# First loads reordered over two queues, the attention state split into two tiles, and a new instruction order in a fused attention and FFN kernel

## The chip, the cores and the metric

The kernel runs on one core of a Trainium2 chip. A core has five engines with instruction streams of their own: TensorE (PE in the profile, with PEld for its weight loads), VectorE (DVE), ScalarE (ACT), GpSimd (POOL) and SyncE (SP). SP, ACT and POOL also issue DMAs; "SPq" and "ACTq" in a timeline are such issues. The metric is the time of one execution on the device in microseconds (us); the time of a kernel is the median of several runs.

## The reference

Four batches, four heads, 1088 tokens, head size 32. The attention is linear: each query and key becomes 64 features, the outer product of two sketches of size 8, and there is no softmax over pairs of tokens. Its output, 4352 tokens of 128 channels, goes through an FFN of 2048 hidden units with a squared relu.

```python
def phi(x):
    a = np.einsum('rd,bhsd->bhsr', S1, x)
    b = np.einsum('rd,bhsd->bhsr', S2, x)
    return np.einsum('bhsi,bhsj->bhsij', a, b).reshape(*x.shape[:-1], r * r)
q_p, k_p = (phi(q), phi(k))
kv = np.einsum('bhsf,bhsd->bhfd', k_p, v)
z = np.sum(k_p, axis=2)
num = np.einsum('bhsf,bhfd->bhsd', q_p, kv)
den = np.einsum('bhsf,bhf->bhs', q_p, z)[..., None] + 1e-06
attn = num / den
...
h = x @ w_in
r = np.maximum(h, 0.0)
g = r * r
return (g @ w_out).astype(np.float32)
```

## The kernel before

**Operations and order.** The kernel first describes its work as named operations (`add`, each with the engines that may run it and the operations it needs). A long text, `PLAN` (lines 31 to 105), then lists every operation once with its engine and, where it needs one, a PSUM bank (`b0` to `b7`), a pair of banks (`h0` to `h6`, where `h0` is banks 0 and 1) or a buffer. `Graph.emit` issues them in that order. So each engine has a fixed list, and runs it strictly in order; semaphores between engines are set automatically from what an operation reads and writes. A DMA that is listed on SP, ACT or POOL is issued when that engine's list gets to it.

**Names.** `S0`, `S1`: loads of the two sketch matrices. `ldk`, `ldq`, `ldv` plus batch: loads of keys, queries, values. `warm`: one small activation that makes ACT load its table. `ST`, `SK`, `SQ0`, `SQ1` (DVE), `SR0`, `SR1` (ACT): the sketch matrices transposed and masked in the forms that later matmuls use. `zero`, `z0`, `z1`, `mk`, `ident`, `iota`: constants and cleared tiles. `heat`: matmuls on zeros that keep TensorE busy until there is data.

**Attention of a batch.** Keys: `tk` (DVE transpose, L393), `ksk` (PE sketches, L400), `kt` (DVE transpose back, L410 and L415), `kp` (feature products on DVE or POOL, L424), `vp` (values copied beside a column of ones, ACT or POOL, L382), `kv` (PE, L436: the state, 64 features by 33 columns for each head, in a PSUM bank). `kve` (L451) copies the state from PSUM into the SBUF tile `st`, in four pieces of 64 partitions: two head positions in each of two arrangements, the second with the partition halves swapped. Queries of batch 0 and of the first part of batch 1: `tq` (DVE transpose, L457), `qr` (PE, L478), `qa` (ACT copy of one factor, L487), `qp` (DVE product, L492), `num` (PE, L521), `mx` (DVE: add eps, reciprocal, multiply; L532 to L535), `tx` (PE transpose, L546), `xe` (copy to `xT`, L551). The rest of the queries go through `qr2`/`qr3` (L562), `ab` (ACT, L567), `rdA` (DMA, L575, the copies named `Aq`), `qb` (PE, L589), `qp` (L596), `den` (PE, L618), `dc` (ACT), `d1` (DMA, L633), `rc` (DVE, L638 and L639), `d2` and `d3` (DMA, L643 and L648, the reciprocals go out to DRAM and come back spread over partitions), `num` (L661) and `xm` (DVE, L668), which writes `xT`.

**FFN.** Ten blocks of tokens (`BLOCKS`: 256, 256, seven of 512, 256). For block n, `m1.n.m` (PE, L697) makes hidden units, `r.n.m` is the relu (ACT, L708, or DVE, L710), `g.n.m` the square (DVE, L721, or ACT, L719), `m2.n.m` (PE, L728) sums over hidden units in a bank, `oe` (DVE, L736) transposes the result into an `osb` buffer, and four `st` DMAs (L746) store it. FFN matmuls of early blocks are interleaved with the attention of later batches.

**POOL.** It clears tiles, waits for a query piece (`gate`, L303), issues the four weight loads (`w_in0`, `w_in1`, `w_out0`, `w_out1`), then runs `vp` and `kp`, and small copies (`gate2`, `pace2k`, `pace3k`) that hold back the loads of the next batch.

Of the kernel before, what the change touches and what calls it, by code (L numbers as in the profile page):

```python
# [36 lines left out]
heat15:PE:b6 heat16:PE:b6 heat17:PE:b6 heat18:PE:b6 heat19:PE:b6 heat20:PE:b6 heat21:PE:b6 heat22:PE:b6
heat23:PE:b6 heat24:PE:b6 heat25:PE:b6 heat26:PE:b6 heat27:PE:b6 heat28:PE:b6 ksk0.0:PE:h0 kt0.0:DVE
heat29:PE:b6 heat30:PE:b6 ksk0.1:PE:h2 ldv0.4:ACT ldv0.5:ACT ldv0.6:ACT ldv0.7:ACT SR0:ACT
SR1:ACT heat31:PE:b6 heat32:PE:b6 heat33:PE:b6 heat34:PE:b6 heat35:PE:b6 heat36:PE:b6 qr0.0:PE:h0:h4  # L40
kt0.1:DVE kp0.0:DVE tq0.8:DVE tq0.16:DVE vp0.0:ACT qa0.0.0:ACT:A0 qp0.0.0:DVE qa0.0.1:ACT:A1
w_in0:POOL w_in1:POOL qr0.8:PE:h2:h6 kv0.0:PE:b0 qp0.0.1:DVE qa0.8.0:ACT:A0 qp0.8.0:DVE qa0.8.1:ACT:A1
qp0.8.1:DVE vp0.4:ACT qr0.16:PE:h1:h3 qa0.16.0:ACT:A1 qa0.16.1:ACT:A0 kp0.7:DVE qp0.16.0:DVE kp0.4:POOL
kv0.4:PE w_out0:POOL w_out1:POOL kv0.7:PE kve0.3:ACT kve0.2:ACT SQ0:DVE gate2:POOL
ldk1.0:SP ldv1.0:SP kve0.1:ACT qp0.16.1:DVE qr0.24:PE:h1:h5 ldv1.1:SP ldv1.2:SP kve0.0:DVE
num0.0:PE:b0 mx0.0:DVE:den0 num0.8:PE:b3 num0.16:PE:b4 tx0.0:PE:b0 qa0.24.0:ACT:A0 qa0.24.1:ACT:A1 qp0.24.0:DVE
qp0.24.1:DVE xe0.0:ACT m1.0.0:PE:h0 mx0.8:DVE:den0 ldv1.3:SP mx0.16:DVE:den1 m1.0.1:PE:h5 tx0.8:PE:b7
xe0.8:DVE r.0.0:ACT:r0 g.0.0:DVE:g0 m1.0.2:PE:h2 tx0.16:PE:b4 xe0.16:DVE r.0.1:ACT:r1 g.0.1:DVE:g1
# [52 lines left out]
m2.8.7:PE g.9.0:DVE:g1 m2.9.0:PE:b5 r.9.2:DVE:r2 r.9.3:DVE:r0 g.9.1:ACT:g0 g.9.2:ACT:g2 m1.9.4:PE:h1  # L101
oe8:DVE:osb0 st8.3584.0:SP m2.9.1:PE m2.9.2:PE g.9.3:DVE:g1 r.9.4:ACT:r1 m2.9.3:PE g.9.4:DVE:g0
m2.9.4:PE st8.3584.1:SP st8.3584.2:SP st8.3584.3:SP oe9:DVE:osb1 st9.4096.0:SP st9.4096.1:SP st9.4096.2:ACT
st9.4096.3:ACT
"""


# [683 lines left out]
```

## Time and profile before

| | |
|---|---|
| three runs, median (lowest to highest) | 111.31 us (110.62 to 111.45) |
| the profiled execution: its time | 112.11 us |
| the profiled execution: span from first to last instruction | 110.1 us |
| first FFN matmul starts | 17.59 us |
| last FFN matmul ends | 105.87 us |
| granted TensorE clock, mean | 1.00 |
| busy: PE, DVE, ACT, POOL | 96.6, 88.8, 85.7, 25.0 us |

A row of a timeline has the start and the time of an instruction (or of a run of like instructions, with their number at the end), the engine, the line, the operation, what it writes and reads and in what shape, and in square brackets how long the engine had stood idle before it and what released it. Matmuls are pipelined and their ends are modelled, so that their rows can overlap. Rows with "q" after the engine are DMA issues or waits of the engine's sequencer.

### The profile page before, as it was taken

To read this page: it belongs to the slowest core of one execution; us is meant where nothing else is said; L and a number is where in the kernel's file an instruction comes from. 1 tells how busy PE (TensorE), PEld (TensorE's weight loads), DVE (VectorE), ACT (ScalarE), POOL (GpSimd) and SP (SyncE) were. 2 spreads that over 40 slices of the span, in tenths; PEclk is the share of its full clock that TensorE was granted. 3 is DMA by queue.
4 is the path that set the end of the run, shared out by engine and by line. 5 is a ranking of instruction groups with operands and counts; after the bars stand their busy time and mean duration, and the time that the engine had idled before them with its cause. 6 is when DMAs were issued, how large, how long until landed. Compare 5 with 4: busy or idle time off the path is not lost.

```text
span 110.1 us, 3711 instructions
## 1 busy us (share of the span) xinstructions
PE 96.6 (88%) x1524; PEld 58.9 (54%) x1539; DVE 88.8 (81%) x153; ACT 85.7 (78%) x108; POOL 25.0 (23%) x37
## 2 busy tenths in 40 slices
PE   5976988998697979997998999999999999999940
PEld 5533976885463546444564543455554554557620
DVE  2479739989997687687959884989998989998940
ACT  2244755998994898899658999999999898999910
POOL 7007700025983990087000000000000000000000
PEclk9999999999999999999999999999999999999999
DMA  0984999931993990964206577005093633502343
GB/s 6 297 192 131 154 187 305 222 129 46 307 270 55 312 261 33 202 131 90 95 10 161 119 191 190 0 6 88 8 227 63 118 53 55 95 6 36 60 85 58
DMA packets 27544, 13.91 MB, mean 126 GB/s; under 512 B 20232, under 2 KB 25352, under 8 KB 27528
## 3 DMA queue, kind: packets, MB, share of 16 engines
q1 hardware_dynamic: 25760, 12.26, 46.4%
q0 software_dynamic: 576, 1.05, 5.8%
q10 hardware_dynamic: 1192, 0.37, 1.4%
q8 instruction: 12, 0.20, 0.7%
q14 instruction: 4, 0.03, 0.1%
HBM read 10.17 MB, written 2.27 MB: 113 GB/s over the span
## 4 chain that ended last, share of the span: by engine, by line
PE 35%; DVE 16%; SPq 13%; issue 11%; DMA 9%; ACT 8%; POOL 4%; DVEq 0%; ACTq 0%
PE psum L697 9%; DVE g L721 8%; SPq L746 8%; PE psum L728 7%; PE psum L436 5%; ACT r L708 5%; PE psum L478 4%; DMA vin<-in_v_dram 4%; PE psum L521 3%; DVE r L710 3%; POOL kp L424 3%; DMA qin<-in_q_dram 3%; PE psum L618 2%; ACT g L719 2%; DMA out_dram<-osb 2%
## 5 line engine op out<-in xcount | busy, mean ns | idle before, releaser
L708 ACT ACTIVATE r<-psum 128x1024 bf16<-128x1024 f32 (+1 forms) x57 | 54.4, 1017 | 5.5 <-PE psum L697 2.8
L697 PE MATMUL psum<-xT,w_in 128*128 128x512 bf16 (+1 forms) x154 | 37.9, 348 | 2.5 <-DVE r L710 1.0
L728 PE MATMUL psum<-g,w_out 128*128 128x512 bf16 (+1 forms) x152 | 38.2, 346 | 1.8 <-DVE st L451 0.6
L721 DVE TENSOR_TENSOR g<-r 128x2048 bf16<-128x2048 bf16 (+2 forms) x31 | 31.8, 1045 | 1.6 <-ACT r L708 0.6
L697 PEld LDWEIGHTS <-w_in 128*128 128x128 bf16 x160 | 21.3, 145 | 14.2 <-issue 3.9
L728 PEld LDWEIGHTS <-w_out 128*128 128x128 bf16 x160 | 14.6, 98 | 14.4 <-issue 3.4
L424 POOL TENSOR_TENSOR kp<-ks 128x768 f32<-128x768 f32 x10 | 16.2, 1632 | 7.1 <-PE psum L697 5.7
L719 ACT ACTIVATE g<-r 128x2048 bf16<-128x2048 bf16 (+1 forms) x10 | 17.4, 1746 | 0.2 <-DVE r L710 0.2
L710 DVE TENSOR_SCALAR r<-psum 128x1024 bf16<-128x1024 f32 (+1 forms) x12 | 14.0, 1175 | 1.4 <-PE psum L697 0.7
L436 PEld LDWEIGHTS psum<-vp,kp 128*32 128x32 f32 (+1 forms) x504 | 7.3, 114 | 4.3 <-issue 3.7
L436 PE MATMUL psum<-vp,kp 128*32 128x33 f32 (+1 forms) x504 | 8.2, 202 | 1.6 <-DVE qp L492 0.7
L492 DVE TENSOR_TENSOR qp<-psum,A 128x256 f32<-128x256 f32 (+2 forms) x14 | 6.2, 474 | 2.4 <-ACT A L487 2.4
L487 ACT COPY A<-psum 128x256 f32<-128x256 f32 (+2 forms) x14 | 5.3, 421 | 2.7 <-PE psum L478 1.7
L293 PE MATMUL psum<-zero 128*128 128x128 bf16 (+1 forms) x36 | 6.0, 347 | 1.3 <-DVE mk L246 1.2
L596 DVE TENSOR_TENSOR qp<-psum,Aq 128x544 f32<-128x544 f32 x8 | 5.4, 719 | 1.6 <-ACT r L708 1.5
L393 DVE STREAM_TRANSPOSE kT<-kin 128x1088 f32<-128x1088 f32 (+2 forms) x5 | 5.4, 1072 | 1.6 <-DMA kin<-in_k_dram 1.6
L736 DVE STREAM_TRANSPOSE osb<-psum 128x512 f32<-128x512 f32 (+1 forms) x10 | 6.2, 625 | 0.5 <-PE psum L728 0.5
L478 PE MATMUL psum<-qT,SR 32*64 32x128 f32 (+2 forms) x224 | 6.1, 304 | 0.6 <-issue 0.4
L457 DVE STREAM_TRANSPOSE qT<-qin 128x1088 f32<-128x1088 f32 (+2 forms) x6 | 5.5, 914 | 0.2 <-DMA qin<-in_q_dram 0.2
L293 PEld LDWEIGHTS <-zero 128*128 128x128 bf16 x37 | 3.7, 135 | 2.7 <-DVE mk L246 1.2
L382 POOL COPY vp<-vin 128x640 f32<-128x640 f32 (+1 forms) x4 | 3.1, 786 | 9.0 <-DMA vin<-in_v_dram 9.0
L478 PEld LDWEIGHTS psum<-qT,SR 32*64 32x64 f32 x224 | 3.5, 131 | 2.8 <-issue 0.9
(58 smaller groups left out, 65.3 us busy)
## 6 DMA issues: line engine op xcount, KB each, us to landing
Aq<-ab SPq DMA_DIRECT2D x16, 136.0 KB, 2.4
kin<-in_k_dram SPq DMA_DIRECT2D x3, 544.0 KB
qin<-in_q_dram SPq DMA_DIRECT2D x3, 544.0 KB
recq<-scd SPq DMA_DIRECT2D x8, 136.0 KB, 2.7
out_dram<-osb SPq DMA_DIRECT2D x16, 64.0 KB, 1.9
vin<-in_v_dram SPq DMA_DIRECT2D x6, 144.0 KB, 5.9
vin<-in_v_dram SPq DMA_DIRECT2D x6, 128.0 KB
w_in<-in_moe_w_in_dram POOLq DMA_DIRECT2D x2, 256.0 KB, 4.7
```

What stands on the lines that cost most here:

```text
L293: nc.tensor.matmul(at(hb)[:, 0:n], zero[:, 0:128], zero[:, 0:n], start=True, stop=True)
L424: eng.tensor_tensor(out=kp[i][:, 4 * a0 : 4 * a1].rearrange("p c (a b) -> p c a b", b=R), in0=t[:, :, 1][:, :, None, :].to_broadcast([128, ...
L436: nc.tensor.matmul(t[p : p + KM, 33 * pr : 33 * pr + 33], kp[i][:, 4 * a0 + 2 * na * pr + 2 * (j - a0) + m, p % 64 : p % 64 + KM], vp[i][: ...
L478: nc.tensor.matmul(at(hbs[h // 2])[p : p + 64, 512 * u + 256 * x : 512 * u + 256 * x + n], SR[32 * h : 32 * h + 32, x, m].rearrange("p a b ...
L492: nc.vector.tensor_tensor(out=qp[i][:, pr, t0 : t0 + 2 * n].rearrange("p (u s) -> p u s", u=2), in0=at(hb).rearrange("p (u s) -> p u s", u ...
L697: nc.tensor.matmul(at(hb)[:, step * w : step * w + N], w_in[:, 128 * E * (ct // E) : 128 * E * (ct // E + 1)].rearrange("p (c e) -> p e c" ...
L708: nc.scalar.activation(o, h, ACTF.Relu)
L710: nc.vector.tensor_scalar_max(o, h, 0.0)
L719: nc.scalar.activation(at(gb)[:, 0 : Q * W * N], r, ACTF.Square)
L721: nc.vector.tensor_tensor(out=at(gb)[:, 0 : Q * W * N], in0=r, in1=r, op=ALU.mult)
L728: nc.tensor.matmul(at(ob)[:, 0:N], w_out[:, ct, :], at(gb)[:, lo : lo + N], start=(ct == 0), stop=(ct == CT - 1))
L746: dma[e].dma_start(out=out[S * b : S * b + S, :].rearrange("(t c) d -> t c d", c=C)[:, c0:c1, 32 * db : 32 * db + 32], in_=at(sbuf)[32 * d ...
```

## The change

Three edits in the program, and a new `PLAN`.

- `S0` is issued on ACT, where `S1` is already; `warm` now comes after both. SP's list begins with the first key piece.
- The state of a batch is two tiles, one for each arrangement, in place of one tile with an axis for it. Each is cleared by its own memset. The copies `kve` are two operations in place of four, one for each arrangement; each is two instructions on the same engine, so that four instructions stay four.
- Two `heat` matmuls fewer (35 in place of 37).
- The operations' order is another one throughout, and so are the PSUM banks. Some operations change engine: `vp0.0` goes from ACT to POOL, `kp0.7` from DVE to POOL, `kp0.4` from POOL to DVE, and some relus, squares and `xe` copies swap between ACT and DVE.

```diff
-N_HEAT = 37
+N_HEAT = 35
...
-    st = [T(f"st{b}", [128, 2, 2, 2 * (D + 1)]) for b in range(B)]
+    st = [[T(f"st{b}_{u}", [128, 2, 2 * (D + 1)]) for u in range(2)] for b in range(B)]
...
-        SU.append(add(f"S{x}", "ACT" if x else "SP", f, kind="dma", kb=8, key="S"))
+        SU.append(add(f"S{x}", "ACT", f, kind="dma", kb=8, key="S"))
...
             for b in range(i, B, NB):
-                nc.gpsimd.memset(st[b], 0.0)
+                for u in range(2):
+                    nc.gpsimd.memset(st[b][u], 0.0)
...
-        for z in range(4):
-            def f_kve(e, z=z):
+        for sw in range(2):
+            def f_kve(e, sw=sw):
                 fn = nc.scalar.copy if e == "ACT" else nc.vector.tensor_copy
-                m, sw = z % 2, z // 2
-                p = 64 * (m ^ sw)
-                o = st[b][p : p + 64, sw]
-                o = o.rearrange("p w (d m) -> p w d m", m=2)[:, :, :, m]
-                fn(o, at(kvb)[64 * m : 64 * m + 64, 0:66].rearrange("p (w d) -> p w d", w=2))
-            o_kve.append(add(f"kve{b}.{z}", "ACT DVE", f_kve, [o_kv, z_ops[i]], uses=[kvb], n=66, kind="cp"))
+                for m in range(2):
+                    p = 64 * (m ^ sw)
+                    fn(st[b][sw][p : p + 64].rearrange("p w (d m) -> p w d m", m=2)[:, :, :, m],
+                       at(kvb)[64 * m : 64 * m + 64, 0:66].rearrange("p (w d) -> p w d", w=2))
+            o_kve.append(add(f"kve{b}.{sw}", "ACT DVE", f_kve, [o_kv, z_ops[i]], uses=[kvb], n=132, kind="kve"))
...
-            o_num = mine("num", add(f"num{b}.{c0}", "PE", f_num, need + [o for z, o in enumerate(o_kve) if z // 2 in sw],
+            o_num = mine("num", add(f"num{b}.{c0}", "PE", f_num, need + [o for z, o in enumerate(o_kve) if z in sw],
```

The other lines that read `st` change only their index. Of the new `PLAN`, here are the lists of the engines as far as the prediction speaks of them (the first line of each pair is the old list).

```text
SP   S0 ldk0.0 ldk0.16 ldq0.0 ldv0.0 ldv0.1 ldv0.2 ldv0.3 ldq0.8 ldq0.16 ...
SP   ldk0.0 ldk0.16 ldq0.0 ldv0.0 ldv0.1 ldv0.2 ldv0.3 ldq0.8 ldq0.16 ...
ACT  S1 warm ldv0.4 ldv0.5 ldv0.6 ldv0.7 SR0 SR1 vp0.0 qa0.0.0 qa0.0.1 qa0.8.0 qa0.8.1 vp0.4 qa0.16.0 qa0.16.1 kve0.3 kve0.2 kve0.1 ...
ACT  S1 S0 warm ldv0.4 ldv0.5 ldv0.6 ldv0.7 SR0 SR1 qa0.0.0 qa0.0.1 vp0.4 qa0.8.0 qa0.8.1 kve0.1 qa0.16.0 qa0.16.1 ...
DVE  zero mk ST SQ1 ident SK tk0.0 tk0.1 tq0.0 kt0.0 kt0.1 kp0.0 tq0.8 tq0.16 qp0.0.0 qp0.0.1 qp0.8.0 qp0.8.1 kp0.7 qp0.16.0 SQ0 qp0.16.1 kve0.0 mx0.0 ...
DVE  zero mk ident tk0.0 ST SK tk0.1 kt0.0 tq0.0 SQ1 kp0.0 kt0.1 SQ0 tq0.8 qp0.0.0 kp0.4 qp0.0.1 qp0.8.0 tq0.16 kve0.0 qp0.8.1 qp0.16.0 mx0.0 qp0.16.1 xe0.0 ...
POOL z0 iota z1 gate w_in0 w_in1 kp0.4 w_out0 w_out1 gate2 vp1.0 pace2k kp1.0 vp1.5 kp1.3 kp1.6 pace3k kp2.0 vp2.0 vp2.5 kp2.6 kp2.3 kp3.0 kp3.6 kp3.3
POOL z0 iota z1 gate w_in0 vp0.0 w_in1 w_out0 kp0.7 w_out1 gate2 vp1.0 vp1.5 pace2k kp1.0 kp1.6 kp1.3 pace3k vp2.0 vp2.5 kp2.0 kp2.3 kp2.6 kp3.6 kp3.0 kp3.3
PE   ... qr0.0 qr0.8 kv0.0 qr0.16 kv0.4 kv0.7 qr0.24 num0.0 num0.8 num0.16 tx0.0 m1.0.0 ...
PE   ... qr0.0 qr0.8 kv0.0 heat34 kv0.4 kv0.7 qr0.16 num0.0 num0.8 qr0.24 tx0.0 m1.0.0 m1.0.1 num0.16 ...
DVE  ... g.1.0 g.1.1 kt1.0 g.1.2 g.1.3 r.2.1 oe0 tq1.0 tk2.0 oe1 kt2.0 g.2.3 ...
DVE  ... g.1.0 xe0.24 kt1.0 g.1.2 g.0.3 r.1.3 oe0 g.1.3 tq1.0 g.2.1 g.2.3 oe1 tk2.0 ...
DVE  ... kve3.0 g.3.5 kve3.2 xm1.18 rc2 ...
DVE  ... g.3.5 xm1.18 g.3.7 rc2 kve3.0 kve3.1 ...
SP   ... ldq2.0 st0.0.0 st0.0.1 st0.0.2 ldk3.0 ldv3.0 st0.0.3 ldv3.1 ldv3.2 ldv3.3 ldq3.0 rdA2.0 d1.1 rdA2.1 d2.1 d3.1 d1.2 rdA3.0 ...
SP   ... ldq2.0 st0.0.0 st0.0.1 st0.0.2 st0.0.3 st1.256.0 ldk3.0 ldv3.0 ldv3.1 ldv3.2 ldv3.3 ldq3.0 rdA2.0 d1.1 rdA2.1 d2.1 rdA3.0 d3.1 d1.2 ...
```

More of the change, by code (lines that the diff above doesn't have):

```diff
@@ L37 @@
[L37 to L48, printed above, removed]
@@ L101 @@
[L101 to L104, printed above, removed]
+ldk0.0:SP zero:DVE z0:POOL iota:POOL mk:DVE S1:ACT ident:DVE tk0.0:DVE
+ldk0.16:SP S0:ACT ST:DVE SK:DVE heat0:PE:b6 heat1:PE:b6 heat2:PE:b6 heat3:PE:b6
+heat4:PE:b6 heat5:PE:b6 heat6:PE:b6 heat7:PE:b6 heat8:PE:b6 heat9:PE:b6 heat10:PE:b6 heat11:PE:b6
```

133 lines of the change are left out of this document (72 added, 61 removed).

## The prediction

> **What bounds the kernel now.** I read the page first, then the busy time by stretches, then the timeline engine by engine where TensorE stands still.
>
> ```profile
> span 110.1 us, 3711 instructions
> ```
> ```profile
> 17.60:60.00 42.40, 37.57 (x900) 24.30 (x909) 36.21 (x65) 35.38 (x46) 18.45 (x15) 1.00 0.62 160
> 60.00:106.00 46.00, 45.10 (x308) 24.72 (x311) 41.29 (x47) 42.72 (x42) 0.00 (x0) 1.00 0.41 83
> ```
>
> Columns of the second fence: stretch, length, busy us of PE, PEld, DVE, ACT, POOL, granted clock, DMA share, GB/s. There are three stages. Up to 17.6 us no FFN matmul runs: latency bounds it. From 60 to 106 us PE idles 46.00 - 45.10 = 0.9 us, and nothing the change reorders there can win more. Between them PE idles 42.40 - 37.57 = 4.83 us, with DVE busy 85% and ACT 83%: what PE waits for there is mostly a step that came late on one of these two. So the time can fall by a shorter start and by less of the 4.83, and in no third way. The granted clock is 1.00 in both, so it plays no part.
>
> The start, on DVE, then on PE:
>
> ```profile
> 4.77 0.71 DVE L393 STREAM_TRANSPOSE kT<-kin 128x512 f32<-128x512 f32 x1 [0.98 <-DMA kin<-in_k_dram]
> 6.10 0.78 DVE L393 STREAM_TRANSPOSE kT<-kin 128x576 f32<-128x576 f32 x1 [0.61 <-DMA kin<-in_k_dram]
> 6.80 0.40 DVE L457 STREAM_TRANSPOSE qT<-qin 128x256 f32<-128x256 f32 x1
> 7.13 0.41 DVE L410 STREAM_TRANSPOSE ks<-psum 128x256 f32<-128x256 f32 x1
> 7.54 0.58 DVE L415 STREAM_TRANSPOSE ks<-psum 128x192 f32<-128x192 f32 x2
> 8.04 1.18 DVE L424 TENSOR_TENSOR kp<-ks 128x1024 f32<-128x1024 f32 x1
> 9.15 0.43 DVE L457 STREAM_TRANSPOSE qT<-qin 128x256 f32<-128x256 f32 x1
> 9.79 0.78 DVE L457 STREAM_TRANSPOSE qT<-qin 128x576 f32<-128x576 f32 x1 [0.21 <-DMA qin<-in_q_dram]
> 10.49 0.38 DVE L492 TENSOR_TENSOR qp<-psum,A 128x256 f32<-128x256 f32 x1
> ```
> ```profile
> 8.46 0.38 PE L293 MATMUL psum<-zero 128*128 128x512 bf16 x1
> 8.77 0.69 PE L478 MATMUL psum<-qT,SR 32*64 32x128 f32 x32
> 9.64 0.70 PE L478 MATMUL psum<-qT,SR 32*64 32x128 f32 x32 [0.18 <-DVE qT L457]
> 11.02 1.13 PE L436 MATMUL psum<-vp,kp 128*64 128x33 f32 x32 [0.69 <-DVE qp L492]
> 12.08 0.69 PE L478 MATMUL psum<-qT,SR 32*64 32x128 f32 x32
> 12.70 1.36 PE L436 MATMUL psum<-vp,kp 128*64 128x33 f32 x40
> 13.99 0.80 PE L478 MATMUL psum<-qT,SR 32*64 32x160 f32 x32
> 15.19 1.63 PE L521 MATMUL psum<-st,qp 128*64 128x66 f32 x48 [0.40 <-DVE st L451]
> 16.84 0.28 PE L546 MATMUL psum<-ident,xs 128*128 128x128 bf16 x2
> 17.59 0.27 PE L697 MATMUL psum<-xT,w_in 128*128 128x256 bf16 x1 [0.46 <-ACT xT L551]
> ```
>
> DVE is without a gap from the second key piece (6.10) on, and the last query transpose, itself waiting for its load at 9.79, stands ahead of the first query product (10.49). PE's first kv matmul (11.02) waits for that product, because both use bank b0; then comes the state copy, and num0.0 waits for that.
>
> **The keys asked for first.**
>
> ```profile
> 0.73 0.80 SPq L239 DMA_DIRECT2D S_sb<-in_S_dram  x1
> 1.60 0.64 SPq L352 DMA_DIRECT2D kin<-in_k_dram  x1
> ```
> ```profile
> 0.74 1.20 ACTq L239 DMA_DIRECT2D S_sb<-in_S_dram  x1
> ```
> ```profile
> 3.12 0.21 DVE L252 STREAM_TRANSPOSE ST<-S_sb 128x32 f32<-128x32 f32 x1 [1.50 <-DMA S_sb<-in_S_dram]
> ```
>
> S0 leaves SP, so every load behind it is issued 1.60 - 0.73 = 0.87 us sooner: both key pieces, all three query pieces, four value pieces. I let them land 0.87 sooner too; the other end is no gain at all, if their queue is full anyway. On ACT, S0 follows S1 at 1.94 and takes 0.80 to 1.20, so it ends by 3.14; S1 ended at 1.94 and ST began 1.18 later, so S0's data are there by 4.3. DVE now does tk0.0 first, from 4.77 - 0.87 = 3.90 to 4.61, and that hides S0; uncovered, its 0.80 to 1.20 would stand ahead of ST and all that uses it. The table load and ACT's four value loads go back by the same 0.80 to 1.20, under the loads of the keys.
>
> **The new order of the start.** DVE has the second key piece at 6.10 - 0.87 = 5.23. Behind it in the new list, by the rows above: 0.78 + 0.41 + 0.40 + two small SQ (0.2 each, taken from the 0.21 of ST) + 1.18 + 0.58 + 0.43 = 4.18, so the transpose tq0.8 ends at 9.41 and qp0.0.0 at 9.79; kp0.4, now on DVE, is three quarters of the 1.18, 0.89, and ends at 10.68. PE: qr0.8 from 9.41, 0.70, to 10.11; kv0.0, 1.13, to 11.24; the new heat34, 0.38, to 11.62; kv0.4 and kv0.7, 1.36, to 12.98. qr0.16 now comes behind them and fills the wait for the state. POOL must keep up:
>
> ```profile
> 8.92 0.36 POOL L303 COPY gate<-qin 128x1 f32<-128x1 f32 x1 [6.04 <-DMA qin<-in_q_dram]
> 9.22 1.26 POOL L308 DMA_DIRECT2D w_in<-in_moe_w_in_dram  x2
> 10.49 1.52 POOL L424 TENSOR_TENSOR kp<-ks 128x768 f32<-128x768 f32 x1
> ```
>
> Gate at 8.92 - 0.87 = 8.05, 0.30 to the next issue, w_in0 0.63 (half of 1.26), vp0.0 at most 1.07 (a row further down), w_in1 and w_out0 0.63 each, kp0.7 two thirds of 1.52 = 1.01. vp0.0 is ready at 10.05, where kv0.0 starts at 10.11; kp0.7 ends at 12.32, where kv0.7, the last 16 of 40 matmuls, starts at 12.44. The cover is a tenth of a us in both. Should the gate stay at 8.92, kv0.0 and all behind it come 0.8 later; I take 0, since the gate's query piece sits behind the same loads, and keep 0.8 for the range. Two state memsets in place of one lie in the 6.04 us in which POOL waits.
>
> **State in two tiles.**
>
> ```profile
> 14.16 0.72 ACT L451 COPY st<-psum 64x66 f32<-64x66 f32 x3 [0.67 <-PE psum L436]
> ```
> ```profile
> 14.91 0.22 DVE L451 COPY st<-psum 64x66 f32<-64x66 f32 x1 [0.81 <-PE psum L478]
> ```
>
> Batch 0's four copies run one after another, 14.16 to 15.13, though the last is on another engine. With a tile for each half, two on ACT and two on DVE can run side by side: 12.98 + 0.1 (14.06 to 14.16 before) + 2 x 0.23 = 13.54; num0.0 at 13.6. From num0.0 to the first FFN matmul was 17.59 - 15.19 = 2.40. tx0.0 now stands behind num0.0, num0.8 (0.54 each, thirds of 1.63) and qr0.24 (0.80), 1.88 instead of 1.63: +0.25. First FFN matmul: 13.6 + 2.65 = 16.25 instead of 17.59, -1.35; num0.16 (0.54) went behind it, so -0.8 in all.
>
> In batches 2 and 3 the same handing over costs PE:
>
> ```profile
> 52.28 0.61 PE L728 MATMUL psum<-g,w_out 128*128 128x512 bf16 x2 [0.63 <-DVE st L451]
> ```
> ```profile
> 59.49 0.44 PE L697 MATMUL psum<-xT,w_in 128*128 128x512 bf16 x1 [0.42 <-DVE xT L668]
> ```
>
> The first waits for a state copy whose bank it takes over; the second for xm1.18, which the old DVE list has behind a state copy of batch 3 and the new one ahead of them. Both together 1.05. Relus on engines that are 83 to 85% busy are the next late thing, so I take half, -0.5 (ends -1.05 and 0).
>
> **POOL against DVE.** An unhindered g of 1024 columns, then one beside POOL's kp:
>
> ```profile
> 19.30 0.68 DVE L721 TENSOR_TENSOR g<-r 128x1024 bf16<-128x1024 bf16 x1
> ```
> ```profile
> 27.21 1.99 DVE L721 TENSOR_TENSOR g<-r 128x1024 bf16<-128x1024 bf16 x1
> 29.13 1.21 DVE L710 TENSOR_SCALAR r<-psum 128x1024 bf16<-128x1024 f32 x1
> ```
> ```profile
> 26.80 1.86 POOL L424 TENSOR_TENSOR kp<-ks 128x768 f32<-128x768 f32 x1 [0.74 <-DVE ks L410]
> 28.61 1.07 POOL L382 COPY vp<-vin 128x512 f32<-128x512 f32 x1
> ```
> ```profile
> 30.39 0.59 PE L697 MATMUL psum<-xT,w_in 128*128 128x512 bf16 x2 [1.04 <-DVE r L710]
> ```
>
> The g started inside the kp and ended at 29.20, 0.54 after it: it ran when POOL was done. The relu behind it came 1.3 late and PE stood 1.04. The new order sets r.2.1 on ACT and takes vp1.5 and the three kp1 in one run. If the collision goes, 1.04 comes back; ACT's row of relus is next late, so -0.7 (ends -1.04 and 0).
>
> [...]
>
> **What else moves.** Some 18 relus and squares swap between ACT and DVE in near equal numbers: nothing by itself. Two heats fewer lie under waits for loads. On SP the Aq copies of batch 3 move ahead of d3.1, whose reciprocals xm1.18 needs:
>
> ```profile
> 57.18 2.53 SPq L575 DMA_DIRECT2D Aq<-ab  x4
> ```
>
> So d3.1 may come up to 2.53 later, and it waits for ab3 too; xm1.18 was late for another reason, so I take 0 and leave part of 2.53 in the upper end. Three stores (st0.0.2, st0.0.3, st1.256.0) move ahead of ldk3.0 and can hold it back behind oe1; ldk3.0 waits for POOL's pace3k in both orders, and pace3k for a load, so 0. The rest of the new order of the middle I take at 0 too: it can remove what is left of the idle time (4.83 - 1.04 - 1.05 = 2.7) or add as much.
>
> **Sum.** -0.8 - 0.5 - 0.7 = -2.0 us. The profiled execution took 112.11 (span 110.1 and 2.0 around it), so 110.1 of its kind; it lay 0.8 above the median 111.31, to which the same -2.0 gives 109.3.
>
> **Rivals.** (1) *Handed back in the middle.* The start comes sooner, but between 17.6 and 60 us ACT and DVE have as much to do as before, and PE waits longer for relus and squares. For it: the 83 and 85%, and 2.0 us are only 41% of PE's 4.83. Against it: DVE also loses waits there. If only a fifth of the sum stays, -0.4: 110.9. (2) *New collisions: slower.* POOL's run vp1.0, vp1.5, kp1.0, kp1.6, kp1.3 is 3 x 1.5 + about 1.5 = 6 us of reading SBUF, and DVE has g.1.2, g.0.3, g.1.3, g.2.1 and g.2.3 about then. A g that starts inside a kp waits up to 1.5, and whatever PE needs behind it waits too, as at 30.39, where 1.3 of delay became 1.04 of PE. It decides from three such on the path on: 3 x 1.04 = 3.1 in place of the 0.7 removed gives back 3.8, time 111.3 + 1.8 = 113.1. For it: five such g. Against it: the old order had one that cost PE in the same place. (3) *The keys land no sooner*, because the transfers and not their issue set it: the start loses 0.87 of its 1.35, the sum is -1.1: 110.2.
>
> **Numbers.** A change of 1% (1.1 us) is about what a measurement here can tell from none. Forecast 0.55, between 108.0 and 110.1 (half of the taken terms more or less); (1) 0.18; (2) 0.17; (3) 0.10, half of it beyond 1%. Faster 0.60, same 0.23, slower 0.17. The range takes in the forecast with 0.6 more gain below (what is left of the idle time), (1) and (3): 107.4 to 111.6; outside stay (2) and a little below.
>
> **What would show it.** First key transpose near 3.9 and first FFN matmul near 16.2 (step 1); state copies of batch 0 on ACT and DVE at once (2); no g of 1024 columns near 2 us and no PE wait of 1 us near 30 (3); PE idle between first FFN matmul and block 5 near 3.5 instead of 4.83. Wrong, if the first FFN matmul is at 16.2 and the span not 1 us shorter (rival 1), if kp and g stretch each other (2), or if the first key transpose is still near 4.8 (3).

## The result, and the profile after

| | before | after |
|---|---|---|
| median of 4 runs each, on one chip (lowest to highest) | 111.38 us (110.62 to 111.64) | 115.03 us (114.12 to 116.36) |
| the profiled execution: time, span | 112.11, 110.1 us | 115.46, 113.4 us |

The change makes the kernel slower: the ratio is 1.028, with a 95% interval from 1.022 to 1.033. Each execution is put down as fast or slow, and this ratio, like every one below, is taken from the fast ones alone (it leaves out the 116.36 us; the others took 114.12 to 115.46), so that it is not the quotient of the medians. The forecast was 109.3 us with a range up to 111.6.

The changed kernel's page begins with its span, and its busy time by stages answers to the two rows that open the prediction:

```profile
span 113.4 us, 3722 instructions
```
```profile
16.60:62.00 45.40, 40.40 (x876) 24.82 (x877) 36.38 (x59) 36.00 (x49) 17.55 (x15) 0.96 0.63 164
62.00:109.00 47.00, 46.52 (x362) 25.35 (x359) 41.58 (x52) 43.41 (x43) 0.00 (x0) 1.00 0.36 73
```

The last stage is as full as before. The loss lies in the middle one: PE idles 45.40 - 40.40 = 5.0 us there (4.83 before, 3.5 expected), and its clock is 0.96 on the mean, by which an estimated 45.40 x 0.04 = 1.8 us of work more are missing.

What follows reads the profile in the order of the prediction's steps. First the start: DVE's timeline of the changed kernel, then the row of its first FFN matmul on PE.

```profile
3.41 0.71 DVE L392 STREAM_TRANSPOSE kT<-kin 128x512 f32<-128x512 f32 x1 [1.11 <-DMA kin<-in_k_dram]
5.24 0.21 DVE L250 STREAM_TRANSPOSE ST<-S_sb 128x32 f32<-128x32 f32 x1 [1.12 <-DMA S_sb<-in_S_dram]
5.49 0.19 DVE L254 TENSOR_TENSOR SK<-ST,mk 128x32 f32<-128x32 f32 x1
```
```profile
16.63 1.07 PE L695 MATMUL psum<-xT,w_in 128*128 128x256 bf16 x8 [0.47 <-DVE xT L549]
```

The first key transpose came 1.36 us sooner (4.77 before). But DVE then stood 1.12 us for S0, and ST, without which no key sketch can be made, came at 5.24 instead of 3.12. The first FFN matmul was still 0.96 us sooner (17.59 before).

The state copies of batch 0, on DVE and on ACT:

```profile
12.99 0.46 DVE L448 COPY st<-psum 64x66 f32<-64x66 f32 x2 [0.36 <-PE psum L435]
```
```profile
13.57 0.44 ACT L448 COPY st<-psum 64x66 f32<-64x66 f32 x2 [1.48 <-DVE st L448]
```

They did not run side by side, although each pair writes a tile of its own: ACT began 0.12 us after DVE's pair had ended, and its wait is put down to DVE's copy.

POOL beside DVE, each on its own timeline:

```profile
26.69 5.35 POOL L423 TENSOR_TENSOR kp<-ks 128x768 f32<-128x768 f32 x3
```
```profile
28.71 1.97 DVE L719 TENSOR_TENSOR g<-r 128x1024 bf16<-128x1024 bf16 x1
```

The collision is still there: a square of 1024 columns takes 1.97 us inside POOL's run of key products (0.68 at 19.35, with POOL idle). What makes it take longer there is not shown.

Where PE waited, by what released it (us in total, times, longest), and three stretches of the busy time (columns as in the prediction's windows):

```profile
PE psum L695 <- DVE xT L666: 2.2, 1, 2.2
...
PE psum L476 <- DVE osb L734: 0.9, 1, 0.9
PE psum L435 <- issue: 0.8, 1, 0.8
```
```profile
33.40:36.80 3.40, 1.70 (x82) 1.03 (x80) 3.37 (x6) 2.40 (x4) 1.47 (x3) 0.98 0.52 96
36.00:37.00 1.00, 0.62 (x43) 0.55 (x43) 1.00 (x3) 0.09 (x1) 0.26 (x1) 0.84 0.72 140
37.00:40.00 3.00, 3.00 (x52) 1.16 (x50) 1.00 (x2) 1.50 (x7) 0.00 (x0) 0.50 1.04 316
```

Two things are new. From 33.4 to 36.8 us PE is busy only half of the time; it waits for an output transpose and for nothing that the profile shows. Right behind, the granted clock falls to 0.50 for three us; in the old profile it was 1.00 throughout. And the longest wait of the middle, 2.16 us, has moved to the scaling xm1.18, ahead of m1.4.0, the first matmul of FFN block 4. Its rows in the changed kernel, with those of SP's queue that lead to it:

```profile
46.96 0.64 PE L616 MATMUL psum<-qp,st 128*32 128x256 f32 x8
...
61.69 0.59 PE L695 MATMUL psum<-xT,w_in 128*128 128x512 bf16 x2 [2.16 <-DVE xT L666]
```
```profile
48.32 1.26 SPq L631 DMA_DIRECT2D d<-dn  x2
...
52.26 0.54 SPq L641 DMA_DIRECT2D scd<-r  x1
52.90 3.33 SPq L573 DMA_DIRECT2D Aq<-ab  x4
56.33 1.97 SPq L646 DMA_DIRECT2D recq<-scd  x4
```
```profile
60.94 0.69 DVE L666 TENSOR_TENSOR xT<-psum,recq 128x512 bf16<-128x512 f32 x1 [2.79 <-DMA recq<-scd]
```

The same steps in the old kernel, on PE, SP and DVE:

```profile
44.03 0.78 PE L618 MATMUL psum<-qp,st 128*32 128x256 f32 x8
```
```profile
45.47 1.19 SPq L633 DMA_DIRECT2D d<-dn  x2
46.70 2.51 SPq L575 DMA_DIRECT2D Aq<-ab  x4
49.32 0.54 SPq L643 DMA_DIRECT2D scd<-r  x1
51.38 1.98 SPq L648 DMA_DIRECT2D recq<-scd  x4
```
```profile
58.74 0.69 DVE L668 TENSOR_TENSOR xT<-psum,recq 128x512 bf16<-128x512 f32 x1
```

This is batch 1's division: den1 on PE, out (d1.1), reciprocal, out (d2.1), back (d3.1), xm1.18. In the changed kernel d3.1 is issued 4.95 us later (56.33 against 51.38). Two causes add up to that. den1 starts 2.93 later (46.96 against 44.03), and between d2.1 and d3.1 lie 4.07 us instead of 2.06, and rdA3.0, 3.33 us of issues, now stands between them: 2.93 + 2.01 = 4.94 (e1 below shows how much of this is rdA3.0's doing). Part of the 2.93 is place and not lateness: m1.3.0, m1.3.1, m1.3.2 and tx1.8 stand ahead of den1 in the new list of PE, and kv2.0 behind it. By the rows of PE (0.43 us for one such m1, 0.63 for the kv) that is an estimated 0.9 us of work. From d3.1's issue to xm1.18 it takes 60.94 - 56.33 = 4.6 us when DVE waits for the data. By that, the old kernel's data were there at about 51.4 + 4.6 = 56.0 and xm1.18 ran at 58.74 for reasons of its own, so the old order had some 2.7 us of slack there. The new one used it up and ran 2.2 us over.

The end can be split at m1.4.0. It starts at 61.69 instead of 59.49, +2.20 us, and from there to the end of the last FFN matmul it takes 47.27 us instead of 46.38, +0.89. (Matmuls' ends are modelled.) Together that is 3.1 of the 3.3 us by which the span is longer.

### The profile page after: what moved, and what is told of

It is laid out like the page before. It is cut to its first block, busy times and chain, and to the rows that moved or that the text cites. A ratio compares the mean times of both kernels' runs of the same rounds, so it can differ in the third digit from the quotient of the medians.

```text
span 113.4 us, 3722 instructions
## 1 busy us (share of the span) xinstructions
PE 100.5 (89%) x1537; PEld 59.4 (52%) x1537; DVE 90.1 (79%) x152; ACT 85.6 (75%) x108; POOL 24.5 (22%) x42
## 4 chain that ended last, share of the span: by engine, by line
PE 43%; DVE 18%; DMA 14%; issue 13%; SPq 4%; POOL 3%; ACT 1%; DVEq 0%; POOLq 0%; ACTq 0%
PE psum L726 18%; PE psum L695 14%; DVE g L719 7%; DMA w_in<-in_moe_w_in_dram 6%; DMA kin<-in_k_dram 5%; DVE r L708 5%; SPq L573 3%; PE psum L476 3%; DMA recq<-scd 3%; DVE qT L455 2%; PE psum L659 2%; PE psum L519 2%; SPq L646 1%; PE psum L435 1%; PE psum L587 1%
## 5 line engine op out<-in xcount | busy, mean ns | idle before, releaser
L695 PE MATMUL psum<-xT,w_in 128*128 128x512 bf16 (+1 forms) x160 | 39.1, 349 | 2.7 <-DVE xT L666 2.2
L726 PE MATMUL psum<-g,w_out 128*128 128x512 bf16 (+1 forms) x160 | 40.1, 350 | 0.4 <-DVE g L719 0.3
L717 ACT ACTIVATE g<-r 128x2048 bf16<-128x2048 bf16 (+1 forms) x12 | 18.6, 1559 | 0.2
L423 POOL TENSOR_TENSOR kp<-ks 128x768 f32<-128x768 f32 (+1 forms) x10 | 15.7, 1590 | 11.9 <-DVE ks L409 6.7
L292 PE MATMUL psum<-zero 128*128 128x128 bf16 (+1 forms) x35 | 6.5, 364 | 1.2 <-DVE mk L244 1.2
L666 DVE TENSOR_TENSOR xT<-psum,recq 128x544 bf16<-128x544 f32 (+1 forms) x5 | 3.4, 712 | 2.9 <-DMA recq<-scd 2.8
L519 PE MATMUL psum<-st,qp 128*32 128x66 f32 (+1 forms) x160 | 4.6, 224 | 0.6 <-ACT st L448 0.5
```

Of the source, the lines that this page charges most:

```text
L292: nc.tensor.matmul(at(hb)[:, 0:n], zero[:, 0:128], zero[:, 0:n], start=True, stop=True)
L423: eng.tensor_tensor(out=kp[i][:, 4 * a0 : 4 * a1].rearrange("p c (a b) -> p c a b", b=R), in0=t[:, :, 1][:, :, None, :].to_broadcast([128, ...
L519: nc.tensor.matmul(t[M * u : M * u + M, 66 * pr : 66 * pr + 66], qp[i][:, pr, t0 : t0 + M], st[b][int(swapped(t0 // 32))][:, pr], start=Tr ...
L695: nc.tensor.matmul(at(hb)[:, step * w : step * w + N], w_in[:, 128 * E * (ct // E) : 128 * E * (ct // E + 1)].rearrange("p (c e) -> p e c" ...
L717: nc.scalar.activation(at(gb)[:, 0 : Q * W * N], r, ACTF.Square)
L726: nc.tensor.matmul(at(ob)[:, 0:N], w_out[:, ct, :], at(gb)[:, lo : lo + N], start=(ct == 0), stop=(ct == CT - 1))
```

## The experiments

Eighteen kernels, in five groups. Each ratio is to the kernel before, run on the same chip in the same group, with its 95% interval. In diffs of the plan only the tokens that moved are shown.

**First: the division and the clock.** The waiting transfer behind rdA3.0 goes back ahead of it (e1); four warming matmul groups bridge PE's hole near 34 us (e2); both (e3); e1 with the output transpose oe1 ahead of the square g.2.3, which it waits for on DVE (e4).

```diff
e1  -d2.1:SP ... rdA3.0:SP ... d3.1:SP
    +d2.1:SP ... d3.1:SP rdA3.0:SP
e2  -qr1.0:PE:h2:h0
    +heat35:PE:b3 heat36:PE:b3 heat37:PE:b3 heat38:PE:b3 qr1.0:PE:h2:h0
e4  -g.2.3:DVE:g2 m1.2.6:PE:h0 m2.1.3:PE oe1:DVE:osb1
    +m1.2.6:PE:h0 m2.1.3:PE oe1:DVE:osb1 g.2.3:DVE:g2      (and e1)
```

> The changed kernel with one move on SP: the four Aq copies of batch 3 (rdA3.0) go behind d3.1 again. Theory: in the changed kernel d3.1 stood behind them and xm1.18 came late, TensorE stood 2.16 us at 61.69; the move takes about 2 us of it away, so some 113.0 us and no TensorE wait over 0.5 us before m1.4.0. Rival: ScalarE and VectorE are behind at that place anyway, and the wait only moves on: 114.5 to 115.

> The changed kernel with four matmuls on zeros of 512 columns ahead of qr1.0, where TensorE stands 0.89 us; they add no dependency. Theory: the granted clock fell to 0.5 from 36.8 to 40.0 us because TensorE was busy only half of the 3.4 us before; with 0.86 us more of work the clock stays at 1.00 and the time falls by 1.1 to 1.7 us, to about 113.5. Rival: TensorE waits for ScalarE and VectorE there, the slow clock is hidden, and the time stays at 115.0; or four are too few and the clock falls all the same.

> Both edits, the move of rdA3.0 and the four matmuls on zeros. Theory: the two losses lie in different places and add up: 115.0 - 2.0 - 1.4 = 111.6, about the time before the change. If this stays at 113 or more, a third loss is still unnamed.

> The changed kernel with rdA3.0 behind d3.1, and the transpose oe1 ahead of the square g.2.3 on VectorE, no added matmuls. Theory: qr1.0 waited for oe1 (its banks), which stood behind two squares of 1.2 us; it now starts some 0.5 us sooner, TensorE's idle stretch shrinks, and whether the clock still falls shows how near the limit this stretch was: 111.3 to 112.0 with the clock at 1.00, 113.0 with it at 0.5.

Measured: e1 1.012 (1.003 to 1.021), e2 1.020 (1.012 to 1.028), e3 1.010 (1.005 to 1.015). e4's four runs went from 113.02 to 116.12 us, too far apart for a ratio; it tells nothing. e1's and e3's intervals lie below that of the change (1.022 to 1.033), e2's does not. By these ratios the exchange of rdA3.0 and d3.1 is a part of the loss: 1.6% between the change and e1, 1.0% between e2 and e3, each give or take about 1. e3 is not back at the old time, so by its own expectation a further loss is still unnamed. In e1, SP's queue and PE's row of m1.4.0 read:

```profile
50.24 0.54 SPq L627 DMA_DIRECT2D scd<-r  x1
53.80 1.74 SPq L632 DMA_DIRECT2D recq<-scd  x4
```
```profile
58.99 0.59 PE L681 MATMUL psum<-xT,w_in 128*128 128x512 bf16 x2 [1.45 <-DVE xT L652]
```

The issue of d3.1 is 2.5 us sooner, m1.4.0 2.7 us sooner, but PE still waits 1.45. Only 0.5 us of the 2.5 can be the edit's. d2.1, which stands ahead of the edit on SP, is itself 2.02 us sooner (50.24 against 52.26), and from d2.1 to d3.1 it takes 3.56 us instead of 4.07. With nothing between the two, SP stood 3.0 us for d2.1's data in e1 (from 50.78 to 53.80; 1.5 us in the old kernel), so d3.1 could not go sooner; e2 and e3 have 4.15 and 3.52 us there. The 2.02 us arose where both kernels have the same lists: in e1's profile the clock stayed at 1.00 from 30 to 42 us, and den1 came at 44.84, 0.81 later than in the old kernel. So the profiles show less gain from this exchange than the ratios do.

In e2 the clock stayed at 1.00 from 30 to 42 us, as expected; but so it did in e1 without the warming matmuls, and e2 does not show that they kept it. PE then waited 2.43 us at m1.4.0, and behind that wait:

```profile
57.00:59.00 2.00, 0.16 (x1) 0.00 (x0) 0.15 (x1) 0.79 (x1) 0.00 (x0) 1.00 0.23 43
59.00:61.00 2.00, 1.41 (x4) 0.61 (x4) 1.97 (x4) 0.38 (x1) 0.00 (x0) 0.66 0.10 16
61.00:63.00 2.00, 2.00 (x7) 0.70 (x5) 0.17 (x1) 1.26 (x2) 0.00 (x0) 0.50 0.12 23
```

The hole and the half clock had only moved there.

**Second: the parts of the change by themselves.** e5 is the changed kernel with ones in place of batch 1's reciprocals. e7 has the new order up to mx0.24 and the old order behind it. e8 is the old kernel with the new order of the first loads alone, e9 the old kernel with the two state tiles alone.

```diff
e5  -in1=rec[i][:, 0 : 2 * n]...
    +in1=(const if b == 1 else rec[i])[:, 0 : 2 * n]...
e8  -S0:SP ... S1:ACT ... ST:DVE SQ1:DVE ldk0.0:SP ... tk0.0:DVE
    +S1:ACT S0:ACT ... ldk0.0:SP ident:DVE tk0.0:DVE ST:DVE SQ1:DVE
e9  -st = [T(f"st{b}", [128, 2, 2, 2 * (D + 1)]) for b in range(B)]
    +st = [[T(f"st{b}_{u}", [128, 2, 2 * (D + 1)]) for u in range(2)] for b in range(B)]
```

> The changed kernel, but the scaling of batch 1's second group of tokens (xm1.18) multiplies by a constant tile of ones instead of the reciprocals that come back from memory; batch 1's division is left out for those tokens, everything else is done. Theory (the chain den1, dc1, d1.1, rc1, d2.1, rdA3.0, d3.1 is what PE stands for): PE no longer waits 2.16 us ahead of m1.4.0; with nothing else late there the whole gain shows, and the time is 112.9 (115.0 - 2.16), ratio to the kernel before near 1.015. Rival (most of that wait hides other lateness, such as kv3.x, num1.18 or the g's of batch 1 being late too): PE waits over 1 us for something else in 57 to 65 us, and the time is 114.2 or more.

> The changed kernel's order up to and including mx0.24 (first key first on SP, both sketch matrices on ACT, two state tiles, merged copies, the new start) and behind it the old kernel's order word for word, on every engine. Theory (the new start is worth its 0.96 us, and what the change lost it lost behind it): the first FFN matmul stays near 16.6, the granted clock stays at 1.00 through 30:42, den1 starts near 43.3, PE's wait at m1.4.0 is 0.5 or less, and the time is 110.4, ratio 0.992 (0.985 to 0.998). Rival (the start's gain is handed back whatever follows it, since batch 1's keys and values come when the weights' gate lets them, 1.2 us later than before): first FFN matmul near 16.6 but the time 111.4 or more, ratio 1.000 or above.

> The old kernel with only the first loads changed: the first keys first on SP, S0 on ACT behind S1, and DVE's order ident, tk0.0, ST. Theory (S0's landing, not the keys, now opens the start): tk0.0 runs near 3.4 instead of 4.77, S0's landing holds ST until about 5.2, SK and ksk0.0 start no earlier than the old 5.54, the first FFN matmul stays at 17.3 to 17.7, and the time is unchanged, ratio 0.997 to 1.003. Rival (the earlier keys are worth what the prediction took, 0.8): first FFN matmul near 16.8 and ratio near 0.993.

> The old kernel with only the state's tile split in two, one for each half; the four copies of each batch out of PSUM stay as they were, three on ACT and one on DVE in batch 0. Theory (it is the PSUM bank that both engines read, not the tile that both write, which keeps the copies apart): DVE's copy kve0.0 still starts only when ACT's kve0.1 has ended (near 14.5), and the time is unchanged, ratio 0.998 to 1.002. Rival (the tile kept them apart, as the prediction had it): kve0.0 starts beside ACT's copies, near 13.5 or before, num0.0 follows 0.3 to 0.8 earlier, and the ratio is 0.993 to 0.997.

Measured: e5 1.019 (1.013 to 1.026), e7 1.006 (1.004 to 1.008), e8 0.999 (0.995 to 1.003), e9 1.003 (0.999 to 1.007).

e7 gave m1.1.1 the pair of banks that still held m1.1.0, so that r.1.0 worked on the other half of the hidden units; e7b below gives it a pair of its own.

e8: theory confirmed. DVE's and PE's rows:

```profile
3.54 0.71 DVE L378 STREAM_TRANSPOSE kT<-kin 128x512 f32<-128x512 f32 x1 [1.32 <-DMA kin<-in_k_dram]
5.70 0.21 DVE L237 STREAM_TRANSPOSE ST<-S_sb 128x32 f32<-128x32 f32 x1 [1.45 <-DMA S_sb<-in_S_dram]
```
```profile
17.56 1.03 PE L682 MATMUL psum<-xT,w_in 128*128 128x256 bf16 x8 [0.46 <-ACT xT L536]
```

The keys are transposed 1.23 us sooner, S0 then lands so late that ST comes 2.58 us later than before, and the first FFN matmul does not move (17.59 before). The earlier loads alone gain nothing; what the new start gained, it gained with its order.

e9: the time is unchanged, as the theory had it. Batch 0 can't tell the bank from the tile, because ACT's last copy (kve0.1) and DVE's copy (kve0.0) write the same one of the two tiles. Batch 2 can: ACT's kve2.1 (51.53 to 51.74) writes the first tile, DVE's next two copies write the second. DVE:

```profile
51.77 0.46 DVE L452 COPY st<-psum 64x66 f32<-64x66 f32 x2 [0.48 <-ACT st L452]
```

DVE waits for ACT's copy although it goes into another tile, as ACT waited for DVE's in the changed kernel. What the copies have in common is the PSUM bank that they read. Releasers come from semaphores, so the trace shows an order that the program keeps; whether the chip could run two such copies at once is not shown. In e9's profile the first FFN matmul came 0.46 us later than in the old one (18.05), and the time was the same, which points to slack behind the start.

e5 took the wait away and won little: from 57 to 65 us PE is busy 7.63 of 8 us instead of 5.84, yet the ratio fell only from 1.028 to 1.019, with intervals that overlap. Its profile lost 1.81 us at another place, a stall told of in the last section, and den1 came at 47.37; so it doesn't show what the wait alone is worth.

**Third: cutting the order in two.** e7b is e7 with a free pair of banks for m1.1.1. e10 is its mirror: old start, new order behind mx0.24. e12 has the new order up to xe1.8 (about 44 us) and the old one behind it. e11 is e3 with ready work put into PE's wait.

```diff
e7b -m1.1.1:PE:h6
    +m1.1.1:PE:h2
e11 -m1.4.0:PE:h6 ... m2.3.3:PE ... m2.3.4:PE ... kv3.6:PE ... m2.3.5:PE
    +m2.3.3:PE m2.3.4:PE kv3.6:PE m2.3.5:PE m1.4.0:PE:h6
```

> As the run before it, the new start up to and including mx0.24 and the old order behind it, but with the second half of the second FFN block (m1.1.1) in a PSUM pair of its own, where the earlier kernel gave it the pair that m1.1.0 still held. Theory (the pair cost it something, and the start's gain is worth nothing behind mx0.24): ratio 1.000 to 1.004, with the first FFN matmul between 16.6 and 17.2. Rival (the shared pair was all that the start lacked): ratio 0.990 to 0.996.

> The mirror of it: the old start up to and including mx0.24, with S0 back on SP's queue, and behind it the changed kernel's order (the two state tiles and merged copies stay in). Theory (all of the loss lies behind mx0.24): ratio 1.020 to 1.035, with PE waiting 1 us or more at xm1.18 and den1 starting near 46 or 47. Rival (the new start harms what follows it, by its later weights' gate and batch 1 loads): ratio 1.010 or less.

> The changed kernel's order up to and including xe1.8 (about 44 us), and the old order behind it, so den1, d1.1, rc1, d2.1 and d3.1 stand where they stood in the old kernel. Theory (two thirds of the loss is the division chain and what stands around it, 44 to 62 us): PE's wait at xm1.18 is below 0.8 us, ratio 1.005 to 1.015. Rival (the loss is made before 44 us): ratio 1.02 or more.

> The kernel with d3.1 ahead of rdA3.0 and four warming matmul groups before qr1.0 (ratio 1.0099), and in addition m2.3.3, m2.3.4, kv3.6 and m2.3.5 put ahead of m1.4.0 on PE, where PE stood 1.6 us for xm1.18. Theory (the stall is plain idle PE, and work that is ready fills it): the wait shrinks by about 1.2 us and the ratio falls to 0.998 to 1.002. Rival (those matmuls are missed later as cover between m1.4.x and its r and g, or their own inputs are late too): ratio 1.006 or more.

Measured: e7b 1.000 (0.996 to 1.004), e10 1.022 (1.017 to 1.028), e12 1.021 (1.013 to 1.029), e11 1.010 (1.006 to 1.014). Here lies the main result. The new start with the old order behind it is worth nothing, although the first FFN matmul came at 16.84 in e7b. The new order behind the old start loses about all that the change loses. And e12, in whose lists den1 and d3.1 stand as in the old kernel, with rdA3.0 behind d3.1, loses about as much. There PE's wait at m1.4.0 was 0.53 us, below the 0.8 that the theory asked for, but the ratio is the rival's: the loss is made before 44 us. With e7b this says where: the new order from mx0.24 to xe1.8 is enough for a loss of 2%, without the exchange on SP. (Orders that are cut and joined are orders of their own; e7b shows that the joint at mx0.24 costs nothing, and for the one at xe1.8 nothing shows it.) e11's median gave no gain over e3.

**Fourth: single pieces of the order between 17 and 44 us.** e13 puts g.2.1 back on ACT, e14 gives POOL its old order for batch 1, e15 joins all repairs, e16 puts g.2.1 on DVE in the old kernel.

```diff
e13 -tq1.0:DVE g.2.1:DVE:g0 ... r.2.4:ACT:r2 r.2.5:ACT
    +tq1.0:DVE ... r.2.4:ACT:r2 g.2.1:ACT:g0 r.2.5:ACT
e14 -vp1.0:POOL vp1.5:POOL pace2k:POOL ... kp1.0:POOL ... kp1.6:POOL ... kp1.3:POOL
    +vp1.0:POOL pace2k:POOL ... kp1.0:POOL vp1.5:POOL kp1.3:POOL kp1.6:POOL
e16 -tk2.0:DVE ... g.2.1:ACT:g2
    +g.2.1:DVE:g2 tk2.0:DVE ...
```

> The changed kernel with one product, g.2.1 (2048 elements), put back on ACT behind r.2.4, where the old kernel had it; the change has it on DVE beside POOL's key products kp1.x. Theory (DVE's two long products beside POOL's keys hold up oe1, qr1.0 and kv1.3, and PE starves from 33 to 37 us): the wait for osb before qr1.0 goes, PE is busy over 2.4 us of 33 to 36, the clock stays at 1.00 there, ratio 1.010 to 1.018 instead of 1.028. Rival (ACT is as late as DVE: g.2.1 now delays r.2.5 and r.2.6 by its 1.9 us): ratio 1.025 or more.

> The changed kernel with POOL's order for batch 1 as it was in the old one: vp1.0, the pacing copy, kp1.0, vp1.5, kp1.3, kp1.6, where the change has both vp first and kp1.6 ahead of kp1.3. Theory (kv1.3 waits for the last of three key products instead of the second): kv1.3 starts up to 1.8 us earlier, ratio 1.015 to 1.022. Rival (kv1.6 then waits as long, and it is DVE and not POOL that is late): ratio 1.025 or more.

> All the repairs together on the changed kernel: d3.1 ahead of rdA3.0, warming matmuls before qr1.0, m2.3.3 to m2.3.5 and kv3.6 ahead of m1.4.0, g.2.1 on ACT, POOL's old order for batch 1. Theory (the loss sits in those five places): ratio 0.995 to 1.003, clock 1.00 in 30 to 42 us. Rival (the order of 17 to 44 us is worse in more than these): ratio 1.006 or more.

> The old kernel with that one product the other way: g.2.1 on DVE, ahead of tk2.0, instead of on ACT. Theory (DVE beside POOL's key products costs): g.2.1 takes 1.8 to 2.5 us where such a product alone takes 1.2, tk2.0 and oe1 come that much later, ratio 1.005 to 1.015. Rival (it has room): ratio 0.998 to 1.002.

Measured: e13 1.026 (1.019 to 1.033), e14 1.025 (1.018 to 1.032), e15 1.019 (1.013 to 1.026), e16 1.004 (1.000 to 1.008), between the two sides of its expectation. No single piece brings the time back, and all together are no better than e1 alone. e14 shows how: in its profile PE's middle was whole again (from 36 to 40 us it is busy 3.68 of 4 us, at clock 1.00), den1 came at 44.44, and PE then stood 2.5 us at m1.4.0, with the clock at 0.79 from 57 to 65 us.

**Fifth: the division by itself.** e18 is the old kernel with d1.1 moved behind rdA2.1. e17 is e3 with the division started sooner and kept free.

```diff
e17 -m1.3.0:PE:h5 ... den1:PE:b7 dc1:ACT
    +den1:PE:b6 dc1:ACT m1.3.0:PE:h5
    -rdA2.0:SP ... d1.1:SP rdA2.1:SP ... rc1:DVE ... d2.1:SP
    +d1.1:SP rdA2.0:SP ... rc1:DVE d2.1:SP rdA2.1:SP tq3.0:DVE
e18 -d1.1:SP rc1:DVE ... rdA2.1:SP qp2.0.1:DVE d2.1:SP
    +rdA2.1:SP d1.1:SP qp2.0.1:DVE rc1:DVE d2.1:SP
```

> The kernel with d3.1 ahead of rdA3.0 and warming matmuls before qr1.0 (ratio 1.0099), with batch 1's division chain started sooner and kept free: den1 and dc1 ahead of m1.3.0, d1.1 ahead of rdA2.0 on SP, rc1 and d2.1 ahead of tq3.0 and rdA2.1. Theory (the chain from den1 to xm1.18, 13.6 to 14.7 us of transfers in every kernel measured, sets when the next FFN block begins, and nothing won before it counts): den1 starts near 44.2 and d1.1 near 45.3 instead of 46.5, the chain ends 1.2 us sooner, PE's wait of 1.60 us at m1.4.0 falls below 0.6, ratio 0.997 to 1.003. Rival (the work that is left behind m1.4.0 is the loss): m1.4.0 starts 1 us sooner, the stretch behind it grows by as much, ratio 1.007 or more.

> The old kernel with the same chain made later by one exchange on SP's queue: d1.1 behind rdA2.1 instead of ahead of it, and rc1 behind qp2.0.1 on DVE so that nothing else waits for it. Theory (the chain bounds the old kernel too, with no slack): d1.1 moves from 45.47 to about 48.1, xm1.18 and m1.4.0 come 2.0 to 2.6 us later, PE waits there for xT, ratio 1.015 to 1.024, about the whole loss of the change. Rival (PE has other work, or the stretch behind it gets shorter by as much): ratio below 1.008.

Measured: e18 1.010 (1.006 to 1.013), e17 1.035 (1.028 to 1.041). e18's rows on SP and PE:

```profile
48.51 1.20 SPq L618 DMA_DIRECT2D d<-dn  x2
51.79 0.35 SPq L628 DMA_DIRECT2D scd<-r  x1
53.38 1.74 SPq L633 DMA_DIRECT2D recq<-scd  x4
```
```profile
59.85 0.87 PE L682 MATMUL psum<-xT,w_in 128*128 128x512 bf16 x3 [0.42 <-DVE xT L653]
```

d3.1 is 2.0 us later and m1.4.0 only 0.36, with the old 0.42 us of wait: the slack of some 2.7 us, worked out above, is there. The ratio still rose by 1%, more than this profile shows, so neither side of the expectation was met. The theory that the division bounds the old kernel falls. In the new order it doesn't hold alone either: in e17 the division came sooner (d3.1 at 53.06, 54.03 in e3), and PE waited for something else:

```profile
49.29 0.36 SPq L628 DMA_DIRECT2D scd<-r  x1
49.70 3.27 SPq L560 DMA_DIRECT2D Aq<-ab  x4
53.06 3.52 SPq L633 DMA_DIRECT2D recq<-scd  x4
```
```profile
57.39 1.14 PE L603 MATMUL psum<-qp,st 128*32 128x272 f32 x16 [1.02 <-DVE qp L581]
```

rdA2.1 (the middle row on SP) is issued 1.9 us later than in e3 (49.70 against 47.80), and batch 2's queries and den2 wait for it. One queue carries all of this, and here what was put first made the rest late.

**The profiles side by side.** In us: start of den1, issue of d3.1, PE's wait at m1.4.0, its start, and the time from there to the end of the last FFN matmul.

| kernel | ratio | den1 | d3.1 | wait | m1.4.0 | from there |
|---|---|---|---|---|---|---|
| before | 1 | 44.03 | 51.38 | 0.42 | 59.49 | 46.38 |
| e7b, new start, old rest | 1.000 | 43.92 | 52.17 | 0.51 | 59.94 | 46.00 |
| e18, old, division late | 1.010 | 43.56 | 53.38 | 0.42 | 59.85 | 46.38 |
| after | 1.028 | 46.96 | 56.33 | 2.16 | 61.69 | 47.27 |
| e1, d3.1 first | 1.012 | 44.84 | 53.80 | 1.45 | 58.99 | 48.38 |
| e2, warming | 1.020 | 44.46 | 54.03 | 2.43 | 59.59 | 48.80 |
| e3, both | 1.010 | 45.01 | 54.03 | 1.60 | 59.32 | 47.53 |
| e14, POOL's old order | 1.025 | 44.44 | 54.02 | 2.53 | 59.67 | 48.80 |
| e11, e3 with the wait filled | 1.010 | 44.46 | 53.30 | none | 58.96 | 46.91 |

With the new order PE waits 1.45 us or more at m1.4.0 in each of these profiles but e11's, and what lies behind takes longer. Two pieces of that can be named. kv3.6 (0.63 us) stands ahead of m1.3.6 in the old plan and behind m1.4.2 in the new one. And in e1 and e3 PE waits once more, 0.98 and 0.48 us near 72 us, for a scaling of batch 2. e11 moved kv3.6 and three FFN groups forward, and the last column fell by 0.62 against e3; but PE then stood 1.17 us at 61.58 for a relu. Its profiled run, 112.38 us, was the fastest of its runs, whose median is 114.08; so the last row shows what the order can reach and not what it mostly does.

No kernel tried beats the old one clear of the noise. What stays open is which moves between mx0.24 and xe1.8 make the loss that e12 shows, and by what, and what makes the remaining 1% of e3. The pieces tried, one after another, only moved PE's wait from 30 to 36 us to 57 to 61 us or back.

## Why the prediction was wrong

- **The rest of the middle at zero (the step that failed).** The prediction took "the rest of the new order of the middle" at 0, though it could remove 2.7 us "or add as much". It was the largest term: e10 has the old start and loses 2.2% all the same, about 2.5 us, and e12, with the new order only as far as xe1.8, loses 2.1%, while the new start with the old order behind it (e7b) loses nothing. So the new order between mx0.24 and xe1.8 alone adds about as much as the 2.7 us that the term named as possible. Which of its moves does so is not shown; the single ones that were tried (e13, e14) gave nothing back beyond their intervals.
- **rdA3.0 ahead of d3.1 at zero.** "Up to 2.53 later" was a fair bound: the step from d2.1 to d3.1 grew by 2.01. But only some 0.5 us of that is rdA3.0's (e1, e3); the rest is that d2.1's data came later than in the old kernel. The term was set to 0 since xm1.18 "was late for another reason". That is true of the old order, where the data had some 2.7 us to spare. In the profiled execution den1 was 2.93 us later as well, and the sum passed the slack; in e1 den1 was only 0.81 later. The ratio fell by 1.6% with the exchange undone (e1), give or take 1. The slack should have been worked out from the rows and weighed against all shifts together.
- **The start, -0.8.** The first FFN matmul came 0.96 us sooner (1.35 was forecast, 0.54 of it paid back behind). The keys landed as forecast or better (3.41 against 3.90), but S0 was there by 5.24 and not "by 4.3", and tk0.0 did not hide it; e8 shows that the loads alone win nothing. What was won is worth nothing: e7b is at 1.000. Of the start, rival (1), handed back in the middle, was right; even a fifth of it was too much.
- **State in two tiles, -0.5, with copies side by side.** Wrong in the mechanism: the copies, which read one PSUM bank, ran one after another with two tiles as well (ACT 0.12 us after DVE's pair in the changed kernel, DVE 0.03 us after ACT's copy in batch 2 of e9). The two waits of PE that the term counted did not both go; the second grew from 0.42 to 2.16.
- **POOL against DVE, -0.7.** The collision stayed (1.97 us beside a key product, 0.68 without one). Rival (2) had the sign and named this run of POOL, but its price, three PE waits of 1.04, is not what came: e14, with POOL's old order, is no faster than the change beyond its interval.
- **The clock, of which it said "it plays no part".** It was 1.00 in the old profile. In the new one it was 0.50 for three us behind a stretch in which PE was half idle. With PE busy all the while, that is an estimated 1.7 us of work (0.16 + 3 x 0.50 + 0.05, from the stretches in the last section). The changed kernel's four runs stand in the order of their granted clocks: 114.12 us at 0.990, 114.60 at 0.987, 115.46 at 0.978, 116.36 at 0.976. Bridging that stretch (e2) did not bring the time back, since the next hole was followed by a fall again (0.50 from 61 to 63 us). It is not the whole loss either: e15's profile has 1.00 throughout, and its ratio is 1.019.

## What to carry to other kernels

Before a transfer is moved ahead of another on a queue, work out how long the data of the one that is pushed back lie ready before they are used, and set against that slack the sum of all shifts that the change makes on the way there, not each by itself. Ask also whether it could have gone sooner at all: here d3.1 stood 3.0 us for d2.1's data with nothing between them (e1). Read two profiles against each other only from the place on where their programs differ; what differs ahead of it is not the change's doing (d2.1 stands ahead of e1's edit and was 2.02 us sooner). A gain at the start of a kernel counts only if nothing behind it waits for something else: the old order behind the new start is the cheap test, and here it showed zero. In a plan where every engine runs a fixed list, expect a new order to move PE's wait rather than remove it, and price "the rest of the order" by the idle time that it can add as well as by what it can remove.
